# Fifteen short series of matmuls of different forms, added behind the last block of a three-stage chain

## The chip, the cores and the metric

The kernel runs on one core of a Trainium2 chip. The number that counts is the device time of one execution in microseconds (us). The engines are named as the profile names them: PE multiplies matrices (PEld is its loading of weights), ACT and DVE work on elements, POOL too, and SP issues the DMA transfers.

## The reference

Three stages follow each other. The first is attention over channels, the other two are gated layers over 12032 tokens of 256 numbers.

```python
B, N, C = (2, 6016, 256)
qn = q / (norm(q, axis=1) + 1e-06)
kn = k / (norm(k, axis=1) + 1e-06)
a = softmax(kn.transpose(0, 2, 1) @ qn / tau)      # 256 x 256, per batch
x = (v @ a).reshape(B * N, C)

h = x @ w_in                                       # 256 -> 2048
x = (h - tanh(h)) @ w_out                          # 2048 -> 256

gate = sigmoid(x @ w_gate)                         # 256 -> 1536
out = (gate * (x @ w_val)) @ w_out2                # 1536 -> 256
```

## The kernel before

The tokens of the two batches are cut into 24 blocks: eleven of 512 tokens and one of 384 in each batch. A block's tokens are the columns of the matmuls, so nearly all of them have 512 columns and those of a batch's last block 384. An accuracy near float32 is reached with operands in two parts: a high part and a low part, both float32r (a float32 that PE takes in one pass), and three products for each tile: high by high, low by high, high by low. So every product of a block stands in the trace as a group of six matmuls with six loads of 128 columns of weights.

The work of a block goes through five kinds of matmul group: `h` (lines L298 to L301, v by the product of attention weights and w_in), `x` (L341 to L344, by w_out), `ga` and `va` (L376 to L379, by w_gate and w_val) and `o` (L405 to L408, by w_out2). ACT and DVE work between them: the tanh polynomial behind `h`, the sigmoid and the product behind `ga` and `va`, and each time the split into parts.

The order on every engine is the order in which the code is written: the kernel switches the scheduler off (`tc.manual_schedule()`) and walks through steps `T`; in each it emits a unit of block p's `h` and `x`, a unit of block p-1's `ga`, `va` and `o`, and whatever else was put down for that step. Behind the last step of the last block only the loop's end follows. There the last `o` group (`p_11`, L405 to L408) is copied out of PSUM, one half by ACT (L419) and one by DVE (L420), and each half is sent to memory by an own transfer (L422). That copy is `ob`.

Pools hand out the tiles. `psw` takes one of four PSUM banks in turn, `rr` one of six float32r tiles, `mk` one of two bf16 tiles, and `v4_p` one of three large tiles for v, converted weights and outputs. A tile that takes the place of an older one waits for whoever still uses that.

At the start, batch 0's attention weights are computed from native float32 operands (L507, L455, 256 columns): the trace shows two matmul records for each such matmul in the code. Batch 1's later tiles of tokens take float32r products of 256 columns (L173 to L175).

Of the kernel before, what the change touches and what calls it, by code (L numbers as in the profile page):

```python
# [15 lines left out]
AX = mybir.AxisListType  # L16

P = 128
# h - tanh(h) = h^3 (C2 ((h^2 + CB)^2 + CG)) to 5e-7 for |h| <= HT; beyond HT the difference itself.
HT = 0.25  # L20
_C0, _C1, C2 = 0.33333317, -0.13328699, 0.051975
CB = _C1 / (2.0 * C2)
# [4 lines left out]
def kernel(  # L27
# [56 lines left out]
    def rr(name, shape=(P, 512)):  # L84
        return rr_p.tile(list(shape), F32R, tag="rr", name=name)
# [7 lines left out]
    make_identity(nc, ident)  # L93

    def warm(n, name):
        """Matmuls that only keep the PE's clock up while it would wait."""
        o = psw(name, (P, P))
        for _ in range(n):
            MM(o, ones, ones, start=True, stop=True)

    aw_hi = [wp.tile([P, NK, 2 * P], F32R, name=f"awh{i}") for i in range(N1 // 2)]
    # until batch 0's a @ w_in is there, its low part's place holds w_in
    win = [wp.tile([P, NK, 2 * P], F32, tag=f"awl{i}", name=f"win{i}") for i in range(N1 // 2)]
    aw_lo = {}
    w1_hi = [wp.tile([P, 2, C], F32R, name=f"w1h{i}") for i in range(N1 // 2)]
# [1 line left out]
    win_d = dr_p.tile([N1 // 2, P, NK, 2 * P], F32, name="win_d")  # L107

    def conv(src, shape, pool, tag, name, w=None, hi=None, lo=None):
        """float64 words to float32 (w), or to its two float32r parts (hi, lo): three stages."""  # L110
        a, m = shape
        st = pool.tile([P, a, 2 * m], U32, tag=tag, name=f"st_{name}")
        nc.sync.dma_start(out=st, in_=src)
        yield
        words = st.rearrange("p a (m t) -> p a m t", t=2)
        low, high = words[:, :, :, 0], words[:, :, :, 1]
        bt = cv(f"cb_{name}", (P, a, m))
        pt = cv(f"cp_{name}", (P, a, m))
        bu, pu = bt.bitcast(U32), pt.bitcast(U32)
        lf = low.bitcast(F32)  # L120
        nc.scalar.activation(bt, high.bitcast(F32), AF.Abs)
        nc.scalar.activation(lf, low, AF.Copy, scale=2.0**-52)
        yield 1
        nc.vector.tensor_scalar(bt, bt, 2.0**-15, 122879.9921875, ALU.max, ALU.min)
        nc.vector.tensor_scalar(
            bu, bu, 0x07FFFFFF, 3, ALU.bitwise_and, ALU.logical_shift_left
        )
        nc.vector.scalar_tensor_tensor(
            out=bu, in0=high, scalar=0xC0000000, in1=bu, op0=ALU.bitwise_and, op1=ALU.bitwise_or
        )  # L130
        nc.vector.tensor_scalar(pu, bu, 0xFF800000, None, ALU.bitwise_and)
        nc.gpsimd.tensor_tensor(out=pt, in0=lf, in1=pt, op=ALU.mult)
        yield
        if w is not None:
            nc.vector.tensor_tensor(out=w, in0=bt, in1=pt, op=ALU.add)
        else:
            nc.scalar.activation(hi, bt, AF.Copy)
            nc.gpsimd.tensor_tensor(out=bt, in0=bt, in1=hi.bitcast(F32), op=ALU.subtract)
            nc.gpsimd.tensor_tensor(out=lo, in0=bt, in1=pt, op=ALU.add)

    def whole(g):
        """Only the stages of conv."""
        for x in g:
            if x is None:
                yield
# [12 lines left out]
        src = words(w_out)[i * 256:(i + 1) * 256, :].rearrange("(a p) d -> p a d", p=P)  # L158
        return conv(src, (2, C), v4_p, "v4", f"w1{i}", hi=w1_hi[i], lo=w1_lo[i])

# [1 line left out]
    kq = {}  # L162
    acc = {}

# [1 line left out]
        kq[b] = psw(f"kq{b}", (P, 2, C))  # L166

    def s_mm(b, hi, lo, first, last):
        """hi, lo: [P, 2 (q, k), C] of one tile of tokens."""
        for ct in range(2):  # L170
            cs = slice(ct * P, (ct + 1) * P)
            o = kq[b][:, ct, :]
            MM(o, hi[:, 1, cs], hi[:, 0, :], start=first and ct == 0, stop=False, skip_group_check=True)  # L173
            MM(o, hi[:, 1, cs], lo[:, 0, :], start=False, stop=False, skip_group_check=True)
            MM(o, lo[:, 1, cs], hi[:, 0, :], start=False, stop=last, skip_group_check=True)  # L175
# [1 line left out]
    aT, nrm, ks = {}, {}, {}  # L177

    def norm_mm(b, sq, sk, first, last):
        """Column sums of the tiles of sq (of q's squares) and sk (of k's), on c's partition."""  # L180
        for o, xs in ((0, sq), (2, sk)):
            for i, x in enumerate(xs):
                for ct in range(2):
                    MM(nrm[b][:, o + ct, :], x[:, ct * P:(ct + 1) * P], ones[:, :NW],
                       start=first and o + i + ct == 0, stop=last and i == len(xs) - 1, skip_group_check=True)

    def s_softmax(b, sq, sk):
        """sq, sk: tiles whose column sums are the sums of squares of q and k."""
        np_ = nrm.get(b)
        if np_ is None:  # L190
            np_ = nrm[b] = psw(f"n{b}", (P, 4, NW))
# [5 lines left out]
        nc.vector.tensor_scalar_add(rn, rn, 1e-6)  # L197
        nc.vector.reciprocal(rn, rn)
        nc.vector.tensor_scalar(rn[:, 2:4], rn[:, 2:4], rtau[:, 0:1], None, ALU.mult)
        # q's factors as rows, the same on every partition: by the ones' product with their diagonal matrix  # L200
        dg = (cv if b else wk)(f"dg{b}", (P, 2, P))
        for ct in range(2):
            nc.vector.tensor_scalar(dg[:, ct, :], ident, rn[:, ct:ct + 1], None, ALU.mult)
# [47 lines left out]
            aT[b] = (hi, lo)  # L251

    def aw_chunk(b, i, w):
        """Rows c of a @ w_in, columns of chunk i."""
        ap_ = psw(f"aw{b}_{i}", (P, 2, 2 * P))
        parts = [(aT[b], w)] if b == 0 else [(aT[b][0], w[0]), (aT[b][1], w[0]), (aT[b][0], w[1])]
        for n, (x, y) in enumerate(parts):
            for ct in range(2):
                for kk in range(2):
                    MM(ap_[:, ct, :], x[:, kk, ct * P:(ct + 1) * P], y[:, kk, :],  # L260
                       start=n + ct + kk == 0, stop=n == len(parts) - 1 and kk == 1, skip_group_check=True)
        yield
        if b == 0:
            aw_lo[i] = wp.tile([P, NK, 2 * P], F32R, tag=f"awl{i}", name=f"awl{i}")
        nc.scalar.activation(aw_hi[i], ap_, AF.Copy)
        nc.vector.tensor_tensor(out=aw_lo[i], in0=ap_, in1=aw_hi[i].bitcast(F32), op=ALU.subtract)  # L266

# [1 line left out]
    vn = {}  # L269

    def load_v(p):
# [76 lines left out]
    def emit_x2(p):  # L348
        n = blocks[p][2]
        xp = xps.pop(p)  # L350
        if p:
            h = one_p.tile([P, 2, TB], F32R, tag="x2h", name=f"x2h{p}")
            lo = one_p.tile([P, 2, TB], F32R, tag="x2l", name=f"x2l{p}")
            h, lo = ([t[:, d, :] for d in range(2)] for t in (h, lo))
        else:
            # block 1's come before the last use of block 0's: these are where aT, acc and s1_split's are at other times
            h = [one_p.tile([P, TB], F32R, tag=t, name=f"x2{t}") for t in ("aT", "acc")]
            lo = [sx_p.tile([P, TB], F32R, tag="sx", name=f"x2l0_{d}") for d in range(2)]
        for d in range(2):
            nc.scalar.activation(h[d][:, :n], xp[d][:, :n], AF.Copy)  # L360
            nc.vector.tensor_tensor(
                out=lo[d][:, :n], in0=xp[d][:, :n], in1=h[d][:, :n].bitcast(F32), op=ALU.subtract
            )
        x2[p] = (h, lo)
# [56 lines left out]
            for d in range(NK):  # L421
                nc.sync.dma_start(out=dst[:, d], in_=o[:, d])  # L422

    # Batch 1's first J0 tiles of tokens, where the PE would wait: native float32 products of
    # what is loaded; their squares are summed later.
    JA, J0, GS = 20, 32, 5
    ks_d = dr_p.tile([2, P, 2 * C], F32, name="ks_d")
    qk1 = [x[1, 0:J0 * P, :].rearrange("(p j) c -> p j c", p=P) for x in (q, k)]
# [33 lines left out]
        nc.scalar.activation(t, epool[0][:, 0:2, :].rearrange("p a c -> p (a c)"), AF.Copy)  # L462
        nc.sync.dma_start(out=ks_d[g], in_=t)

# [1 line left out]
    rtau = const.tile([P, 1], F32, name="rtau")  # L466
    cb_t = const.tile([P, 1], F32, name="cb")
    ct_t = const.tile([P, 1], F32, name="ct")
# [10 lines left out]
    with tc.tile_pool(name="boot1", bufs=1) as boot1, tc.tile_pool(name="boot4", bufs=4) as boot4, \  # L479
# [28 lines left out]
                       start=j + jj == 0 and ct == 0, stop=j + jj == NT - 1, skip_group_check=True)  # L508

        def boot_squares(i):  # L510
            """Squares, summed in accb; the last chunk's are left to the matmuls."""
            j, n = chunks[i]
            raw = raws.pop(i)
            sq = boot3.tile([P, 2, JB, C], F32, tag="sq", name=f"sq{i}")
# [11 lines left out]
        wait, live = {}, []  # L526

        def load(i):
            """Chunk i of q and k, and what of w_in is converted along with it."""
            if i < NCH:  # L530
                load_raw(i)
            if i in (2, 5, 8, 11):
# [21 lines left out]
        nc.scalar.activation(dummy, ones[:, 0:1], AF.Sqrt)  # L554
        while live:
            live = [g for g in live if next(g, live) is None]
        # the softmax's stages, and in between what does not wait for them: two of w_in's
        # conversions, v's first parts, batch 1's first products
        sm0 = s_softmax(0, *sq)
        tv = split_v(0)  # L560
        for step in (tail[0], sm0, sm0, tail[0], sm0, tv, e_mm, e_mm, e_mm, sm0, sm0, tv, tail[1],
# [19 lines left out]
            h, lo = ((wg_hi[i], wg_lo[i]), (wv_hi[i], wv_lo[i]))[which]  # L581
        return conv(src, (2, 2 * P), v4_p, "v4", f"m{which}{i}", hi=h, lo=lo)

# [1 line left out]
    sraw = {}  # L585

    def s1_load(j):
# [40 lines left out]
        nc.vector.tensor_tensor(out=ks[1], in0=ks[1], in1=t, op=ALU.add)  # L628

    def s1_sum():  # L630
        """The sum over a group of tiles to that over all."""
        nc.vector.tensor_tensor(out=ks[1], in0=ks[1], in1=kq[1], op=ALU.add)

# [1 line left out]
    bg = {}  # L635

    def at(step, fn, *a):
        bg.setdefault(step, []).append((fn, a))

    # GV0: the steps of block 0's column tiles of w_gate and w_val; OFF..: those of the others', from  # L640
    # the first step of the block after
    GV0 = (20, 21, 22, 24, 25, 27, 28, 30, 31, 33, 34, 35)
    OFF1 = (4, 5, 7, 8, 9, 11, 12, 13, 14, 15, 16, 17)
    OFFS = (3, 4, 5, 7, 8, 9, 11, 12, 13, 15, 16, 17)
# [58 lines left out]
    for T in range(-4, (NB + 1) * N1 + 18):  # L703
# [42 lines left out]
                emit_out(u[0])  # L746
        if e0 and e0[1] == (4 if T < N1 else 12) and e0[0] + 1 < NB:
            load_v(e0[0] + 1)
    ms.__exit__(None, None, None)


# [31 lines left out]
```

## Time and profile before

| what | value |
|---|---|
| time, median of 2 runs | 2437.05 us (2436.18 to 2437.92) |
| profiled execution, span from first to last instruction | 2436.4 us |
| PE busy in the span | 2372.4 us, 97% |
| DVE, ACT, POOL busy | 1841.3 us, 1606.9 us, 259.6 us |
| mean granted TensorE clock | 0.991 |

The span stands 0.65 us under the median of the runs, within what the two runs differ by (1.74 us). For the profiled execution no other time than its span is given, so differences in the span are taken as differences in the time. Matmul records overlap: a record of 512 columns is about 0.39 us long, and the next begins 0.23 us after it. So what a matmul costs is read from start to start, or from a count over a stretch without gaps, not from the length of its record.

### The profile page before, as it was taken

Reading aid. Unit: us, or ns where it says so; the run is one execution under the profiler, and the core shown is the slowest. Engines: PE = TensorE matmul, PEld = TensorE weight load, DVE = VectorE, ACT = ScalarE, POOL = GpSimd, SP = SyncE. Lnnn points to the kernel's source line nnn. Section 1 sums busy time; section 2 is a strip of 40 time slices with the busy share of each in tenths; the row PEclk is TensorE's granted clock in tenths of the full one; section 3 lists DMA queues with packets and bytes.
Section 4 is the critical chain, followed back from the end, with each engine's and each line's share of the span. In section 5 each row is a group of like instructions: output and inputs, shape, how many; then the busy total and the mean of one; then the engine's idle time right before and its main releaser. Section 6 shows DMA issues by size and latency. Waiting matters only on the chain.

```text
span 2436.4 us, 29276 instructions
## 1 busy us (share of the span) xinstructions
PE 2372.4 (97%) x10408; PEld 1935.4 (79%) x10408; DVE 1841.3 (76%) x2791; ACT 1606.9 (66%) x2820; POOL 259.6 (11%) x171
## 2 busy tenths in 40 slices
PE   7868899999999999999999999999999999999999
PEld 6656678878888888788888888888888888888888
DVE  7899977778777777777777777777777777777764
ACT  4766666676766676776666766666666666666663
POOL 6466600111100000000000000000000000000000
PEclk9899999999999999999999999999999999999999
DMA  7432210111110110000100000000000000000000
GB/s 280 139 117 96 74 35 22 39 35 31 52 35 5 44 35 5 18 10 10 44 5 18 16 1 18 18 1 18 18 1 18 18 1 18 18 1 16 1 9 16
DMA packets 49106, 82.62 MB, mean 34 GB/s; under 512 B 4416, under 2 KB 18496, under 8 KB 48960
## 3 DMA queue, kind: packets, MB, share of 16 engines
q1 hardware_dynamic: 48960, 80.76, 10.0%
q8 instruction: 81, 1.33, 0.2%
q14 instruction: 65, 0.53, 0.1%
HBM read 65.80 MB, written 14.94 MB: 33 GB/s over the span
## 4 chain that ended last, share of the span: by engine, by line
PE 87%; DVE 7%; issue 3%; ACT 2%; POOL 1%; DMA 0%; SPq 0%; DVEq 0%; POOLq 0%; ACTq 0%
PE h L298 7%; PE x L344 7%; PE h L301 7%; PE h L299 7%; PE x L342 6%; PE x L341 6%; PE o L406 5%; PE o L405 5%; PE ga L377 5%; PE o L408 5%; PE ga L376 5%; PE va L377 5%; PE va L376 5%; PE va L379 5%; PE ga L379 5%
## 5 line engine op out<-in xcount | busy, mean ns | idle before, releaser
L314 DVE SCALAR_TENSOR_TENSOR w<-u,h 128x512 f32<-128x512 f32 (+1 forms) x384 | 259.1, 675 | 345.5 <-ACT t L310 345.1
L309 ACT ACTIVATE u<-h 128x512 f32<-128x512 f32 (+1 forms) x384 | 223.4, 582 | 256.7 <-PE h L301 256.4
L317 DVE COPY_PREDICATED w<-m,t 128x512 f32<-128x512 uint16 (+1 forms) x384 | 318.3, 829 | 41.0 <-DVE w L316 1.8
L298 PE MATMUL h<-vTh,awh 128*128 128x512 f32 (+1 forms) x768 | 303.8, 396 | 2.7 <-DVE t L315 1.9
L299 PE MATMUL h<-vTh,awl 128*128 128x512 f32 (+1 forms) x768 | 301.0, 392 | 4.2 <-DVE awl L266 4.2
L312 ACT ACTIVATE s<-u,cb 128x512 f32<-128x512 f32 (+1 forms) x384 | 274.0, 713 | 0.0
L313 ACT ACTIVATE m<-u,ct 128x512 bf16<-128x512 f32 (+1 forms) x384 | 272.3, 709 | 0.0
L316 DVE SCALAR_TENSOR_TENSOR w<-s,w 128x512 f32<-128x512 f32 (+1 forms) x384 | 264.3, 688 | 0.0
L315 DVE TENSOR_TENSOR t<-h,t 128x512 f32<-128x512 f32 (+1 forms) x384 | 258.0, 672 | 0.0
L301 PE MATMUL h<-vTl,awh 128*128 128x512 f32 (+1 forms) x768 | 237.6, 391 | 0.0
L310 ACT ACTIVATE t<-h 128x512 f32<-128x512 f32 (+1 forms) x384 | 223.7, 582 | 3.5 <-DVE w L314 0.8
L377 PE MATMUL va<-x2h,wvl 128*128 128x512 f32 (+1 forms) x552 | 216.2, 392 | 0.0
L377 PE MATMUL ga<-x2h,wgl 128*128 128x512 f32 (+1 forms) x552 | 216.1, 392 | 0.0
L376 PE MATMUL ga<-x2h,wgh 128*128 128x512 f32 (+1 forms) x552 | 215.9, 391 | 0.1
L376 PE MATMUL va<-x2h,wvh 128*128 128x512 f32 (+1 forms) x552 | 215.8, 391 | 0.0
L388 DVE TENSOR_TENSOR sg<-va,sg 128x512 f32<-128x512 f32 (+1 forms) x288 | 191.9, 666 | 19.7 <-PE va L379 18.8
L387 ACT ACTIVATE sg<-ga 128x512 f32<-128x512 f32 (+1 forms) x288 | 168.8, 586 | 16.6 <-PE ga L379 12.5
L379 PE MATMUL va<-x2l,wvh 128*128 128x512 f32 (+1 forms) x576 | 178.5, 391 | 0.0
L379 PE MATMUL ga<-x2l,wgh 128*128 128x512 f32 (+1 forms) x576 | 178.0, 390 | 0.0
L298 PEld LDWEIGHTS h<-vTh,awh 128*128 128x128 f32 x768 | 145.2, 189 | 36.6 <-DVE t L315 4.4
L299 PEld LDWEIGHTS h<-vTh,awl 128*128 128x128 f32 x768 | 144.9, 189 | 35.9 <-DVE awl L266 7.5
L301 PEld LDWEIGHTS h<-vTl,awh 128*128 128x128 f32 x768 | 144.2, 188 | 33.3
(396 smaller groups left out, 4772.0 us busy)
## 6 DMA issues: line engine op xcount, KB each, us to landing
v<-in_v_dram SPq DMA_DIRECT2D x22, 512.0 KB, 4.2
out_dram<-ob SPq DMA_DIRECT2D x22, 512.0 KB, 3.0
sr<-in_q_dram SPq DMA_DIRECT2D x47, 128.0 KB, 2.3
sr<-in_k_dram SPq DMA_DIRECT2D x47, 128.0 KB, 2.6
raw<-in_q_dram SPq DMA_DIRECT2D x13, 384.0 KB, 8.1
raw<-in_k_dram SPq DMA_DIRECT2D x13, 384.0 KB, 8.2
st_wi<-in_moe_w_in_dram SPq DMA_DIRECT2D x8, 512.0 KB, 7.3
er<-in_q_dram SPq DMA_DIRECT2D x16, 256.0 KB, 2.6
```

Source lines behind the costliest of these rows:

```text
L298: MM(o[:, :n], aw_hi[i][:, kk, fs], h[:, kk, :n], start=kk == 0, stop=False)
L299: MM(o[:, :n], aw_lo[i][:, kk, fs], h[:, kk, :n], start=False, stop=False)
L301: MM(o[:, :n], aw_hi[i][:, kk, fs], lo[:, kk, :n], start=False, stop=kk == 1)
L312: nc.scalar.activation(s, u, AF.Square, bias=cb)
L313: nc.scalar.activation(m, u, AF.Relu, bias=ct2)
L314: nc.vector.scalar_tensor_tensor(out=w, in0=u, scalar=C2, in1=hp, op0=ALU.mult, op1=ALU.mult)
L315: nc.vector.tensor_tensor(out=t, in0=hp, in1=t, op=ALU.subtract)
L316: nc.vector.scalar_tensor_tensor(out=w, in0=s, scalar=CG, in1=w, op0=ALU.add, op1=ALU.mult)
L317: nc.vector.copy_predicated(w, m.bitcast(U16), t)
L376: MM(o[:, :n], wht[m // 2][:, d, ms], h[d][:, :n], start=d == 0, stop=False)
L377: MM(o[:, :n], wlt[m // 2][:, d, ms], h[d][:, :n], start=False, stop=False)
L379: MM(o[:, :n], wht[m // 2][:, d, ms], lo[d][:, :n], start=False, stop=d == 1)
```

## The change

Behind the loop, 172 matmuls in fifteen series are added, fourteen of 12 and one of 4. They read weights that are in SBUF anyway, a bf16 tile of ones, a float32r tile of zeros and a float32 tile of 0.5; they write to banks of `psw`, and nothing reads these sums. Three instructions prepare the tiles: two memsets on DVE and one Copy with scale 0 on ACT. The other edits remove comments and docstrings. The output is computed as before.

```diff
         if e0 and e0[1] == (4 if T < N1 else 12) and e0[0] + 1 < NB:
             load_v(e0[0] + 1)
+
+    bones = mk_p.tile([P, 512], BF16, tag="mk", name="bones")
+    nc.vector.memset(bones, 1.0)
+    zero = rr("zero")
+    nc.scalar.activation(zero, bones, AF.Copy, scale=0.0)
+    flat = lambda t: t.rearrange("p a c -> p (a c)")
+    mv = [flat(w1_hi[0]), flat(w1_lo[0]), flat(w2_hi[0]), flat(w2_lo[0])]
+    wt = [wg_hi[0][:, 0, :P], wg_lo[0][:, 0, :P], wv_hi[1][:, 1, :P], wv_lo[1][:, 1, :P]]
+
+    def probe_same():
+        o = psw("probe_same")
+        for i in range(12):
+            MM(o, wt[0], mv[0], start=i == 0, stop=i == 11)
+
+    def probe_turns():
+        o = psw("probe_turns")
+        for i in range(12):
+            MM(o, wt[i % 4], mv[i % 3], start=i == 0, stop=i == 11)
+
+    def probe_banks():
+        o = [psw("probe_banks") for _ in range(2)]
+        for i in range(12):
+            MM(o[i % 2], wt[i % 4], mv[i % 3], start=i < 2, stop=i > 9)
+
+    def probe_bf16():
+        o = psw("probe_bf16")
+        for i in range(12):
+            MM(o, bones[:, :P], bones, start=i == 0, stop=i == 11)
+
+    def probe_rows64():
+        o = psw("probe_rows64")
+        for i in range(12):
+            MM(o[:64], wt[i % 4][:, :64], mv[i % 3], start=i == 0, stop=i == 11)
+
+    def probe_rows32():
+        o = psw("probe_rows32")
+        for i in range(12):
+            MM(o[:32], wt[i % 4][:, :32], mv[i % 3], start=i == 0, stop=i == 11)
+
+    def probe_zero():
+        o = psw("probe_zero")
+        for i in range(12):
+            MM(o, zero[:, :P], zero, start=i == 0, stop=i == 11)
+
+    def probe_cols(n):
+        o = psw(f"probe_cols{n}")
+        for i in range(12):
+            MM(o[:, :n], wt[i % 4], mv[i % 3][:, :n], start=i == 0, stop=i == 11)
+
+    def probe_later(n):
+        o = psw(f"probe_later{n}")
+        for i in range(12):
+            MM(o[:, :n], wt[i % 4], mv[i % 3][:, 512 - n:], start=i == 0, stop=i == 11)
+
+    def probe_native():
+        o = psw("probe_native")
+        for i in range(4):
+            MM(o, ones, flat(vn_probe)[:, :512], start=i == 0, stop=i == 3)
+
+    vn_probe = v4_p.tile([P, NK, 512], F32, tag="v4", name="vprobe")
+    nc.vector.memset(vn_probe, 0.5)
+    probe_same()
+    probe_turns()
+    probe_banks()
+    probe_bf16()
+    probe_rows64()
+    probe_rows32()
+    probe_zero()
+    for n in (504, 500, 480, 448, 400, 320):
+        probe_cols(n)
+    probe_later(496)
+    probe_native()
     ms.__exit__(None, None, None)
```

On PE the series stand behind the last `o` group and ahead of the branch that ends the program; shown is the start of them. A name ahead of the arrow is the tile written, those behind it are the operands, and the last number is the output's size.

```order
 L406 MATMUL o_21170<-p_11h,w2l_573 128x384
 L408 MATMUL o_21170<-p_11l,w2h_567 128x384 x2
-L779 UNCONDITIONAL_BRANCH
+L761 MATMUL probe_same<-w1h_116,wgh_538 128x512 x12
+L766 MATMUL probe_turns<-w1h_116,wgh_538 128x512
+L766 MATMUL probe_turns<-w1l_124,wgl_544 128x512
+L766 MATMUL probe_turns<-w2h_562,wvh_551 128x512
+L766 MATMUL probe_turns<-w1h_116,wvl_557 128x512
```

Nothing ahead of the last `o` group changes its place on PE; the series take the place directly behind it. On DVE, where both memsets are added, the end of the program reads so:

```order
 L323 TENSOR_TENSOR p_11l<-sg_11_21447,p_11h 128x384
 L420 COPY ob_21460<-o_21170 128x384
-L779 UNCONDITIONAL_BRANCH
+L751 MEMSET bones 128x512
+L809 MEMSET vprobe 128x1024
+L851 UNCONDITIONAL_BRANCH
```

Both memsets come behind the copy of the last output's second half (L420), so that the copy and its transfer keep their places.

## Rows read from the trace of the kernel before

**Rows 1.** The page: busy time of PE, and its slices of the span.

```profile
PE 2372.4 (97%) x10408; PEld 1935.4 (79%) x10408; DVE 1841.3 (76%) x2791; ACT 1606.9 (66%) x2820; POOL 259.6 (11%) x171
...
PE   7868899999999999999999999999999999999999
...
PEclk9899999999999999999999999999999999999999
```

**Rows 2.** The chain that ended last, its end: start us, us, what.

```profile
2430.45 0.53 ACT p_11h L322
2430.98 0.04 issue
2431.02 0.44 PE o L405
...
2431.99 0.36 PE o L408 x2
2432.35 0.02 issue
2432.37 0.50 ACT ob L419
2432.87 0.02 issue
2432.89 0.56 DVE ob L420
```

**Rows 3.** Timeline of all engines, the last instructions: start us, us, engine, line.

```profile
2431.82 0.51 PE L408 MATMUL o<-p_11l,w2h 128*128 128x384 f32 x2
...
2432.89 0.94 SPq L422 DMA_DIRECT2D out_dram<-ob  x2
2432.89 0.56 DVE L420 COPY ob<-o 128x384 f32<-128x384 f32 x1 [1.34 <-ACT ob L419]
```

**Rows 4.** DMA from 2430 to 2437 us: busy tenths in 40 slices.

```profile
DMA  0000000000000000000004994997000000000000
```

**Rows 5.** Stretches: us, busy (x count) of PE, PEld, DVE, ACT, POOL; PEclk; DMA.

```profile
1800.00:2000.00 200.00, 200.00 (x862) 161.55 (x861) 146.19 (x226) 130.97 (x228) 0.00 (x0) 1.00 0.03 11
2000.00:2200.00 200.00, 200.00 (x861) 161.57 (x860) 145.93 (x226) 131.34 (x228) 0.00 (x0) 1.00 0.03 11
2400.00:2430.00 30.00, 30.00 (x175) 30.00 (x174) 10.54 (x20) 9.64 (x19) 0.00 (x0) 1.00 0.00 1
```

**Rows 6.** Timeline of PE in the last block, columns as in rows 3.

```profile
2424.38 0.34 PE L376 MATMUL ga<-x2h,wgh 128*128 128x384 f32 x1
...
2427.50 0.34 PE L376 MATMUL ga<-x2h,wgh 128*128 128x384 f32 x1
```

**Rows 7.** Timeline of PE, six float32r matmuls of 256 columns and the one behind.

```profile
656.28 0.28 PE L173 MATMUL kq<-sh 128*128 128x256 f32 x1
...
656.99 0.40 PE L298 MATMUL h<-vTh,awh 128*128 128x512 f32 x1
```

**Rows 8.** Timeline of PE, native float32 matmuls of 256 columns, equal ones merged.

```profile
4.37 2.05 PE L507 MATMUL kq<-raw 128*128 128x256 f32 x4 [0.81 <-DMA raw<-in_k_dram]
...
46.73 1.67 PE L507 MATMUL kq<-raw 128*128 128x256 f32 x7
62.77 1.94 PE L184 MATMUL n<-ones,accb 128*128 128x64 f32 x8 [14.37 <-DVE accb L523]
...
70.27 2.77 PE L455 MATMUL kqe<-er 128*128 128x256 f32 x6
```

**Rows 9.** Stretches round the pause of PE at 48 us, and at the end.

```profile
53.00:62.00 9.00, 0.00 (x0) 0.00 (x0) 8.83 (x12) 4.48 (x6) 2.80 (x2) 0.50 0.45 166
70.20:72.90 2.70, 2.70 (x9) 2.16 (x8) 1.96 (x4) 2.69 (x6) 0.00 (x0) 0.50 0.00 0
2433.00:2435.00 2.00, 0.00 (x0) 0.00 (x0) 0.45 (x1) 0.00 (x0) 0.00 (x0) 1.00 0.53 197
2435.20:2436.40 1.20, 0.00 (x0) 0.00 (x0) 0.00 (x0) 0.00 (x0) 0.00 (x0) 0.50 0.00 0
```

**Rows 10.** Groups by line, a memset on DVE: count, busy us, mean ns.

```profile
L91 DVE MEMSET ones<- 128x128 f32 x1 | 0.2, 165 | 0.8 <-PEq L765 0.8
```

## The prediction

> **What bounds the kernel now.** I read the page first: PE is busy for 97% of the span and at the full clock but for the first slices [rows 1]. For this change only the end counts, so I went on to the chain of waits there. It runs through the last `o` group on PE, the copy of its first half by ACT and of its second by DVE [rows 2]. Behind that copy comes the second transfer, and DMA is busy until slice 28 of 40, about 2435.0 us [rows 4]; the span ends at 2436.4. So 1.4 us of waits and barrier follow the last transfer. On PE the two last matmuls begin at 2431.82 and, since a record of 384 columns is 0.34 us long and both together take 0.51, at 2431.99 [rows 3, 6]. Their step, start to start, is 0.173 us (below), so PE could begin another matmul at 2432.17. From there to the span's end it has 4.2 us in which it does nothing.
>
> **What the change does to that end.** Nothing ahead of the last `o` group moves, and the output's copies and transfers stand ahead of the new DVE and ACT instructions. So the output leaves as before. The 172 new matmuls begin at 2432.17, and the program's end waits for PE's last instruction as for that of every engine. The first 4.2 us of them are hidden behind the output's way out, and the rest lengthens the span one to one. The price is thus the sum of the steps.
>
> **The steps.** In the two dense stretches nearly all matmuls have 512 columns; 200 us hold 862 and 861 records, one of which began earlier, hence 200/861 = 0.2323 us each [rows 5]. In the last block the 18 matmuls from one `ga` group to the next take 2427.50 - 2424.38 = 3.12 us, 0.1733 us at 384 columns [rows 6], as 30/174 = 0.172 says too [rows 5]. Six float32r matmuls of 256 columns take 656.99 - 656.28 = 0.71 us, 0.118 us each [rows 7]. Native float32 at the full clock: seven records take 1.67 us, of which the last is about 0.38, so the step is 1.29/6 = 0.215 us [rows 8]. The first chunk holds one tile of tokens, two matmuls in the code, and shows four records [rows 8]; a native matmul of 256 columns thus costs two records, 0.430 us, and one of 512 columns twice that, 0.860 us.
>
> **The sum.**
> The series of 512 float32r columns with 128 output rows and full weights (same, turns, banks, zero) are 48 matmuls at 0.2323: 11.15 us. That weights are the same each time, banks change or operands are zero shows in no row; I take the body's step for all, and 0.215 (512 columns streamed as the native records do it) as the lower end.
> Those with 64 and 32 output rows are 24 more at 0.2323: 5.58 us. No row of the trace has fewer than 128 output rows. Below lies again 0.215, above the native price 0.860; I take the body's, since the same 512 columns are streamed and the trace prices by columns.
> The six column counts: between the three measured steps I draw straight lines. That gives 0.146 for 320, 0.181 for 400, 0.203 for 448, 0.218 for 480, 0.227 for 500 and 0.229 for 504, together 1.202 us, times 12: 14.43 us. The twelve matmuls of 496 columns from a later start cost 0.225 each: 2.70 us.
> The bf16 series: no bf16 matmul is in the trace. I take 0.215, the step of a record that streams 512 columns in two passes: 12 x 0.215 = 2.58 us. Half of that (0.118, as many bytes as 256 float32r columns) is the lower end; 0.2323 with a weight load of 0.118 that isn't hidden (rows of 256 columns show loads no slower than that), 0.35 or 4.2 us in all, the upper.
> The native series is 4 x 0.860 = 3.44 us.
> Together 11.15 + 5.58 + 14.43 + 2.70 + 2.58 + 3.44 = 39.9 us. PE's last record ends some 0.16 us behind its step (0.34 against 0.173), at 2432.17 + 39.9 + 0.16 = 2472.2. Behind it comes the barrier. In the profile of before, 1.4 us lie between the last transfer's landing and the end; a part of that is the queue's check of transfers that are then long done, so between 0.6 and 1.4, and I take 0.9. The new span is 2473.1 us, 36.7 longer. With the median of the runs instead of the span: **2473.8 us**, a factor of 1.015.
>
> **What I cost at nothing.** The two memsets take about 0.3 to 0.7 and 1.3 us, by 0.165 us for 128 columns [rows 10], and run from 2433.45, when DVE has copied `ob` [rows 2]. They are needed by the bf16 series after 36 matmuls, at about 2440.5, and by the native one at about 2469; ACT's Copy is needed by the zero series, near 2449. The cover is 6 us or more. If it were gone, PE would wait 2 us at most. Each series takes a bank of `psw` that a series or group four banks back wrote, so its first matmul waits for a matmul that ended at least two series before. I cost this at nothing; were the pipeline emptied each time, it would cost up to 0.16 us (record less step) at eleven places, 1.8 us. The clock stays up: in 30 us of the last block it is 1.00 with PE busy throughout [rows 5], and it fell only after PE had stood idle from 2432.3 to past 2435.0 [rows 9].
>
> **The rivals.**
> *The step of the body is not that of the series.* In the body ACT and DVE read and write beside PE; behind the last block they are idle. If the 0.2323 us were theirs, the series would run at 0.215 per 512 columns, 0.42 ns a column: 72 matmuls 15.5, the column counts 13.4, the later start 2.5, with bf16 and native 37.4 us in all, 2.5 less: 2471.3 us. Against it: in the last block ACT and DVE are busy a third of the time instead of two thirds [rows 5], and 384 columns still cost 0.1733, 0.45 ns a column. The Trainium skill ("TensorE: Matmul & The Clock Gate", section on the back-to-back issue gap) gives columns / 2.4 GHz plus 2.5 ns, 0.2158 us for 512 columns, without naming the operand's type; the native records agree with that, the float32r rows of the body do not, and by the page alone the time would be this rival's.
> *A slow form.* This one ends more than 2% slower. All float32r rows before have 128 output rows and 256, 384 or 512 columns. If those with 64 and 32 rows were taken at the native price, 24 x (0.860 - 0.232) = 15.1 us are added: 2488.9 us, 2.1% over before. If it were the column counts that are no multiple of 128, then 12 x (2652 + 496) columns at 1.68 ns (0.430 / 256) make 63.5 us in place of 17.1: 2520 us. It decides from one such pair of series on. For it speaks only that no row excludes it; against it, that the trace prices three column counts near one line.
> *The half clock.* After 14.4 us of idleness PE's clock was 0.50, the 1.2 GHz level, and native records then came (2.77 - 0.63)/5 = 0.427 us apart instead of 0.215 [rows 8, 9]. Were the series to run so, the sum would double to 79 us: about 2513 us. Against it: PE would have to stand idle first, and the longest cover that could break is the 2 us above.
> *Pauses between the series.* Emptied pipelines and late semaphores at the eleven bank waits, 0.16 to 0.4 us each, add 2 to 4 us: 2476 to 2478.
> *Not slower.* If the unread sums were left out, or the program's end did not wait for PE, the time stays 2437. The built program has all series in PE's order, ahead of the branch.
>
> **How the numbers follow.** Sum as worked out 0.68; body's step not that of the series 0.12; pauses 0.10; slow form 0.06; half clock 0.02; not slower 0.02. The first three end between 2471 and 2478, which is the range. About 2% either way, 48.7 us, is what a measurement of this kernel can tell from no change; the first three and the last are within it. Slower by more than 2% is a slow form or the half clock, 0.08; faster by more than 2% has no mechanism, and gets 0.01; within 2% gets 0.91. The forecast itself is a time 1.5% longer, inside that bound.
>
> **What would show it.** In the profile after: the first of the series begins within 0.1 us of 2432.17; the copies and transfers of `ob` stand where they stood; PE has no idle time over 0.1 us before a series, and the clock is 1.00 until the end; 11 steps of a 512-column series take 2.56 us; a series of 320 columns 1.6 us, one of bf16 2.4 us; from the end of the last record to the end of the span 0.6 to 1.4 us. The prediction is wrong if one of the forms unseen before (64 or 32 rows, bf16, odd column counts) has a step far from its line, or if the ends of the span are set by something other than PE.

## The result and the profile after

The kernel with the fifteen series takes 2474.45 us (median of two runs, 2474.05 and 2474.86) against 2437.05: a ratio of 1.0149, 95% interval 1.013 to 1.0168, so 37.4 us more. Forecast were 2473.8 us, between 2471 and 2478.

The page of the kernel after, the same parts as in [rows 1]:

```profile
PE 2412.7 (98%) x10584; PEld 1965.7 (80%) x10584; DVE 1843.9 (75%) x2793; ACT 1610.5 (65%) x2821; POOL 259.9 (11%) x171
...
PEclk9899999999999999999999999999999999999999
```

PE is busy 40.3 us longer (2412.7 - 2372.4), and its clock stays up to the end. The records grew by 176: 168 of fourteen series, and eight for the four native matmuls.

The chain that ended last in the kernel after (start us, us, what) answers to [rows 2]:

```profile
2431.20 0.35 PE o L408 x2
2431.54 2.81 PE probe_same L761 x12
2434.35 2.78 PE probe_turns L766 x12
2437.13 2.79 PE probe_banks L771 x12
2439.92 2.60 PE probe_bf L776 x12
2442.53 2.78 PE probe_rows L781 x12
2445.30 2.77 PE probe_rows L786 x12
2448.07 2.74 PE probe_zero L791 x12
2450.81 14.44 PE probe_cols L796 x72
2465.25 2.71 PE probe_later L801 x12
2467.96 3.43 PE probe_native L806 x8
```

Before, the chain went from the last `o` group to the copies by ACT and DVE; now it stays on PE. Between the fifteen series there is no "issue" piece, so no pause. Added up they take 39.85 us, and the last one ends at 2471.39; the span ends 0.9 us later, at 2472.3. That the end waits for PE stands among the waits of the queue that issues the transfers (us in total, times, longest); before, that queue's wait at the end was for the output's transfer alone, 1.5 us:

```profile
SPq L851 <- PE probe_native L806: 36.3, 1, 36.3
```

The timeline of the same kernel round the last `o` group answers to [rows 3]:

```profile
2431.03 0.51 PE L408 MATMUL o<-p_11l,w2h 128*128 128x384 f32 x2
2431.38 2.97 PE L761 MATMUL probe_same<-w1h,wgh 128*128 128x512 f32 x12
...
2432.10 1.37 SPq L422 DMA_DIRECT2D out_dram<-ob  x2
2432.11 0.56 DVE L420 COPY ob<-o 128x384 f32<-128x384 f32 x1 [1.33 <-ACT ob L419]
...
2433.36 0.91 DVE L809 MEMSET vprobe<- 128x1024 f32 x1 [0.16 <-issue]
```

The first series follows the last `o` matmul after a step of 0.18 us (2431.38 - 2431.20), the copy and the transfers of `ob` keep their distance to it, and the three preparing instructions end at 2434.3, over 5 us ahead of their first use at 2439.8. All of it stands 0.8 us earlier than in the profile of before, which is the difference of two executions: behind the same `o` group, the stretch to the span's end was 4.4 us and is now 41.1 (2472.3 - 2431.20), forecast 41.1 (0.17 + 39.9 + 0.16 + 0.9).

### The profile page after: what moved, and what is told of

Same layout as the page of the kernel before. It is cut to its first block, busy times and chain, and to the rows that moved or that the text cites. A ratio compares the mean times of both kernels' runs of the same rounds, so it can differ in the third digit from the quotient of the medians.

```text
span 2472.3 us, 29636 instructions
## 1 busy us (share of the span) xinstructions
PE 2412.7 (98%) x10584; PEld 1965.7 (80%) x10584; DVE 1843.9 (75%) x2793; ACT 1610.5 (65%) x2821; POOL 259.9 (11%) x171
## 4 chain that ended last, share of the span: by engine, by line
PE 87%; DVE 6%; issue 3%; ACT 2%; DMA 1%; POOL 1%; SPq 0%; DVEq 0%; POOLq 0%; ACTq 0%
PE h L298 7%; PE h L299 6%; PE h L301 6%; PE x L344 6%; PE x L342 6%; PE x L341 6%; PE o L406 5%; PE ga L377 5%; PE o L405 5%; PE ga L376 5%; PE va L376 5%; PE va L377 5%; PE va L379 5%; PE o L408 5%; PE ga L379 5%
## 5 line engine op out<-in xcount | busy, mean ns | idle before, releaser
L317 DVE COPY_PREDICATED w<-m,t 128x512 f32<-128x512 uint16 (+1 forms) x384 | 318.7, 830 | 41.1 <-DVE w L316 1.8
L298 PEld LDWEIGHTS h<-vTh,awh 128*128 128x128 f32 x768 | 145.1, 189 | 36.7 <-DVE t L315 4.4
```

The costliest lines, as they stand in the source:

```text
L298: MM(o[:, :n], aw_hi[i][:, kk, fs], h[:, kk, :n], start=kk == 0, stop=False)
L317: nc.vector.copy_predicated(w, m.bitcast(U16), t)
```

## Experiments

**e1_same12 and e2_same24: how much of PE's work the end hides.** Only the first series stands behind the last block, with 12 or with 24 matmuls.

```diff
     ms.__exit__(None, None, None)   # of the kernel before, ahead of it:
+    o = psw("probe_same")
+    for i in range(12):             # e2: 24
+        MM(o, wt[0], mv[0], start=i == 0, stop=i == 11)
```

> Only the series with one pair of operands stands behind the last block: 12 matmuls, 2.8 us. Theory (PE's free 4.2 us at the end hide the first matmuls): PE ends ahead of the last transfer, the stretch from the last o matmul's start to the span's end stays 4.4 us, and the time stays within 1 us of 2437.05. Rival (each added matmul lengthens the time, because the program's end waits for PE on its own): 7.2 us for that stretch, and 2.8 us more.

> The same series with 24 matmuls, 5.6 us, longer than the 4.2 us that PE has free. Theory: from the last o matmul's start to the span's end 0.17 + 24 x 0.2323 + 0.16 + 0.9 = 6.8 us instead of 4.4, so 2.4 us more. Rival (one to one): 10.0 us and 5.6 more. If all unread matmuls were free: 4.4.

Measured: e1 1.0003 of the kernel before (0.9994 to 1.0012), e2 1.0009 (1.0 to 1.0018). The timeline of e1, and then that of e2, whose spans are 2436.5 and 2438.9 us:

```profile
2431.86 0.51 PE L408 MATMUL o<-p_11l,w2h 128*128 128x384 f32 x2
2432.20 2.97 PE L756 MATMUL probe_same<-w1h,wgh 128*128 128x512 f32 x12
```

```profile
2431.89 0.52 PE L408 MATMUL o<-p_11l,w2h 128*128 128x384 f32 x2
2432.25 5.79 PE L756 MATMUL probe_same<-w1h,wgh 128*128 128x512 f32 x24
```

In e1 PE ends at 2435.17, about when the output's second transfer lands (2435.0 by the DMA slices), and the end comes 1.3 us later: from the last `o` matmul's start (2432.03) to the span's end 4.4 us, as without the series. In e2 PE ends at 2438.04 and the end follows 0.9 us later: 6.8 us (2438.9 - 2432.07), as worked out. So matmuls behind the last block are free as long as PE's end and the 0.9 us behind it stay within the output's way out, and from there cost one to one. Of e2's 5.62 us, 2.4 us lengthened the span, so 3.2 us were hidden. One to one from the first on is refuted; the times, 0.1 and 2.1 us over before, say the same.

**e3_twice: the sum doubled.**

```diff
+    for _ in range(2):
     probe_same()
...
     probe_native()
```

> All fifteen series twice over. Theory (the steps add up and nothing else counts): the second pass costs its full 39.9 us, 2474.45 + 39.9 = 2514.4 us, with the clock at 1.00 throughout. Rival (part of the price was paid once: a start, an end, pauses at the first use of a form): less than 2512. Rival (a longer run of such matmuls brings the clock down): more than 2520.

Measured: 2514.03 us, 1.0313 (1.0299 to 1.0327), 39.6 us over the kernel with one pass; 2514.4 were expected. In the chain of e3 the second pass begins at 2471.80 and its last series ends as follows:

```profile
2471.80 2.81 PE probe_same L761 x12
...
2508.24 3.43 PE probe_native L806 x8
```

2508.24 + 3.43 - 2471.80 = 39.87 us. Nothing was paid only once, and the clock stayed at 1.00.

**e4_in_the_pause: matmuls where PE waits.**

```diff
+                warm(60, "warm1")
                 nrm[0] = psw("n0", (P, 4, NW))
                 norm_mm(0, *([accb[:, x, 0]] for x in range(2)), True, False)
```

> The kernel before with 60 unread matmuls of ones (native float32, 128 columns, about 12.9 us) put not at the end but where PE waits 14.4 us for DVE at 48 us. Theory (a matmul costs what PE's exposed time costs): nothing is added, PE still goes on at 62.8 us, and since it did not stand idle the clock stays at 1.00 there instead of 0.50 from 52.6 to 73.1 us, which takes 1 to 3 us off: 2434 to 2437. Rival (any 13 us of PE work is added to the time): 2450. Rival (the pause was not free, for instance because SBUF or the queue is shared): over 2439.

Measured: 2436.8 us, 0.9997 (0.9988 to 1.0006). PE's timeline in e4, beside [rows 8]:

```profile
49.35 13.56 PE L99 MATMUL warm<-ones 128*128 128x128 f32 x120
63.13 1.08 PE L184 MATMUL n<-ones,accb 128*128 128x64 f32 x8 [0.22 <-DVE accb L523]
```

13.6 us of added PE work cost nothing that can be measured: PE still goes on when DVE is done, 0.36 us later than in the profile of before, and the next eight matmuls take 1.08 us instead of 1.94, at a granted clock of 0.98 between 62.7 and 68 us instead of 0.50. The expectation that the clock stays up was met only in part: PE waited again for 2.3 us, and the clock was 0.50 from 68 to 70 us in e4 too, and 0.79 from 70 to 73 (0.50 before). What all this gave back, 1.1 us at the first token product (77.33 instead of 78.41), is less than the interval. The rivals of 2450 and of over 2439 fall.

**e5_forms: values or type.** The prediction priced the bf16 series apart from the others. Eight series of 24 with other values show why it is shorter.

```diff
+    series("d_ones", lambda i: (one[:, :P], one))
+    series("d_nil", lambda i: (nil[:, :P], nil))
+    series("d_nilw", lambda i: (nil[:, :P], mv[0]))
+    series("d_nilx", lambda i: (wt[0], nil))
+    series("d_bf16", lambda i: (bw[:, :P], wide))
```

> Eight series of 24 matmuls of 512 columns behind the last block, each with other values or another type: real weights and tokens' factors (d_same), float32r ones (d_ones), float32r zeros (d_nil), zero weights with real moving data (d_nilw), real weights with zero moving data (d_nilx), bf16 copies of real data (d_bf16), real data on 64 input rows (d_half), weights and moving data of one tile (d_own). The question is what makes a float32r step of 512 columns 0.232 us where the bf16 series had 0.216. Theory (the type does): all float32r series 0.226 to 0.235, bf16 with real data 0.216. Rival (the values do, and bf16 was short for its ones): d_ones and d_nil near 0.216, d_bf16 with real data near 0.232. Rival (two tiles read at once get in each other's way): d_own, d_ones and d_nil short, the others long.

The chain of e5 (start us, us of 24 matmuls):

```profile
2432.87 5.62 PE d_same L767 x24
2438.50 5.45 PE d_ones L767 x24
...
2449.39 5.44 PE d_nilw L767 x24
2454.83 5.62 PE d_nilx L767 x24
2460.45 5.20 PE d_bf L767 x24
2465.64 5.80 PE d_half L767 x24
2471.44 5.68 PE d_own L767 x24
```

This kernel and those of e6, e8 and e10 to e12 were timed once each, so only steps within their profiles are read, at a granted clock of 1.00. Per step: 0.234, 0.227, 0.227 (d_nil), 0.227, 0.234 and, for bf16 with real data, 0.217 with a first step of 0.227 and then 0.216. So the type makes 0.011 us, and values make nothing: zeros as moving data with w_gate's weights cost as much as real ones, and zero weights as little as ones. Two tiles read at once are not the cause either: d_nilw reads two and has the short step. The last two series begin with a step of 0.34 us, where the number of input rows changes from 128 to 64 and back; behind it d_half has 0.234, so half the input rows save nothing, and d_own 0.228. That left 0.007 us between series of the same type, for which the place of the operands was a suspect.

**e6_narrow: fewer columns.**

```diff
+    for n in (288, 256, 224, 192, 160, 128, 64, 384, 512):
+        cols(n)          # 24 matmuls each
```

> Nine series of 24 float32r matmuls with other column counts than the change had. Theory (the price goes by columns down to the weights' load, which is a floor): 288 columns 0.132 us, 256 columns 0.118, and 224, 192, 160, 128 and 64 columns all about 0.108 to 0.12, the time in which 128 columns of weights load. Rival (columns alone): 0.104, 0.090, 0.076, 0.062 and 0.034 us. Rival (a slow form under 256 columns, at the native price): 192 columns 0.32 us.

Stretches of e6 from the first matmul of 224 and of 64 columns to the next series (us, PE busy, PEld busy):

```profile
2437.66:2440.33 2.67, 2.67 (x27) 2.67 (x25) 0.00 (x0) 0.00 (x0) 0.00 (x0) 1.00 0.00 0
2448.32:2450.97 2.65, 2.65 (x27) 2.65 (x26) 0.00 (x0) 0.00 (x0) 0.00 (x0) 1.00 0.00 0
```

By 24: 0.111 and 0.110 us; 256 columns took 0.118 and 288 took 0.132. From 224 columns down to 64 the step stays at 0.111. That the load of 128 columns of weights is this floor was argued and is not shown: PEld is busy all the time, but so it is at 288 columns, above the floor, and no series had few columns and fewer weights. Columns alone and the slow form are refuted.

**e7_align and e8_starts: the start within 64 bytes.** The weights of w_gate, w_val and w_out2 and v's parts begin 32 bytes off a multiple of 64, since a small tile of 32 bytes stands before them; w_out's and the zeros don't.

```diff
-        rn = one_p.tile([P, 4], F32, tag="rn", name=f"rn{b}")
+        rn = one_p.tile([P, 16], F32, tag="rn", name=f"rn{b}")[:, :4]
```

> The kernel before without any added series; one small tile (rn, four numbers a partition) takes 64 bytes instead of 32, so that the tiles behind it (v's parts and the weights wgh to w2l), which began 32 bytes off a multiple of 64, begin at multiples of 64. Theory (where a float32r operand's bytes begin sets 3 to 11 ns of a 512-column step, as the forms' series showed 0.227 us with weights that begin at such a multiple and 0.231 to 0.238 with those that don't): the body's 8334 steps of 512 columns, 0.2327 us on average, come down to between 0.227 and 0.230, 22 to 47 us less, 2390 to 2416 us. Rival (the place in memory counts in another way, or the weights' slices do): 2436 to 2439, unchanged. Rival (PE's gain is eaten by waits for DVE): above 2425 with PE idle time grown.

> Nine series of 24 float32r matmuls of 480 columns behind the last block, all of two tiles that begin at multiples of 64 bytes; weights and moving data begin 0, 4, 8 or 16 numbers (0, 16, 32, 64 bytes) into them (w0x0, w4x0, w8x0, w16x0, w0x4, w0x8, w0x16, w8x8), and one has 32 output rows (m32). Theory (32 bytes off a multiple of 64 is the cost): w0x0, w16x0 and w0x16 0.212 to 0.214 us flat, w8x0 and w4x0 0.216 to 0.220, w0x8 and w0x4 longer too or equal. Rival (it is the distance of the two tiles, not the start): all alike. m32: if the load of 128 columns of weights makes the 10 ns that are left over the 0.216 of bf16 (0.203 at 480 columns), then near 0.204, else as w0x0.

e7 measured 2432.84 us, 0.9979 (0.997 to 0.9988): faster, clear of noise, but by 5 us and not by 22 to 47. A stretch of its body beside [rows 5]:

```profile
1800.00:2000.00 200.00, 200.00 (x863) 161.92 (x862) 145.44 (x224) 131.04 (x227) 0.00 (x0) 1.00 0.03 11
```

200/862 = 0.2320 us a step instead of 0.2323. In e8 the 480-column series took 0.216 to 0.220 us wherever they began, with 32 output rows too (5.20 us for 24), although a load of 32 columns has a record of 108 ns instead of 188. The theory that the start within a tile costs 3 to 11 ns fell, and the load as the cause of the remaining 0.011 us with it.

**e9_both: the pause filled and the tile of 64 bytes.** The edits of e4 and e7 together.

> The kernel before with the 60 matmuls of ones in PE's pause and the small tile of 64 bytes together, no series at the end. Theory (each takes its own: 1 us by the clock after the pause, 5 us by shorter steps): 2431 to 2433 us against 2438. Rival (the start is held by other engines and the pause's gain was noise): as with the tile alone, 2432.8.

Measured: 2431.92 us, 0.9974 (0.9965 to 0.9984). That is faster than both kernels; beyond e7 alone it is 0.0005 of the time, within the intervals, so that the two gains add is not shown.

**e10_pairs and e11_align_series: distance, place or alternation.**

```diff
+    for a, c in ((0, 0), (0, 1), (0, 2), (0, 3), (0, 4), (0, 6), (4, 4), (4, 5), (4, 6), (4, 0)):
+        series(f"p{a}w{c}", w1_hi[c], w1_hi[a])
+    series("far", aw_hi[0], w1_hi[0])
+    series("far2", wg_hi[0], w1_hi[4])
```

> Twelve series of 24 float32r matmuls of 512 columns behind the last block. Moving data is the first or the fifth tile of w_out's high parts (2048 bytes apart each), weights come from the same or another tile of them (p0w0, p0w1, p0w2, p0w3, p0w4, p0w6, p4w4, p4w5, p4w6, p4w0), or from far ones (far: attention product's, far2: w_gate's). What is open is why a step is 0.2266 us in some series and 0.231 to 0.238 in others with the same values and type, now that the start within 64 bytes is out. Theory (the distance between the two tiles): p0w0 as p4w4, p0w1 as p4w5, p0w2 as p4w6, with p0w0 at 0.2266 and others longer. Rival (the weights' place alone): p0w4 as p4w4, p0w6 as p4w6, p0w0 as p4w0. Rival (neither; the phase at which a series begins): no such pairs, and changes inside a series.

> The kernel with the small tile of 64 bytes, so that w_gate's tiles begin at multiples of 64, and seven series of 24 matmuls of 512 columns behind it: one pair of w_out's tiles (a_one, again at the end as a_last), w_gate's weights with the same moving data (a_gate), two weights in turn (a_wts of w_out, a_gwts of w_gate), two moving tiles in turn (a_mov), and the change's four weights and three moving tiles in turn (a_turn). Theory (the start of the weights within 64 bytes sets the step as long as one pair repeats, and the alternation of tiles sets it otherwise, so that the body gained little by the alignment): a_one, a_gate, a_last 0.2267, a_wts, a_gwts, a_turn 0.230 to 0.233. Rival (w_gate's place in memory, not its start): a_gate 0.231 to 0.238 as before, a_wts 0.2267. Rival (the start alone): all seven 0.2267.

The chain of e10, all pairs of w_out's tiles merged by the moving tile, and then four series of e11's chain:

```profile
2431.72 32.68 PE p0w L755 x144
2464.39 21.76 PE p4w L755 x96
```

```profile
2427.67 5.46 PE a_one L755 x24
2433.13 5.59 PE a_gate L755 x24
2438.71 5.46 PE a_wts L755 x24
...
2455.22 5.51 PE a_turn L755 x24
```

The timeline of e10, its last series:

```profile
2491.43 5.78 PE L755 MATMUL far<-w1h,wgh 128*128 128x512 f32 x24
```

In e10 every pair takes 0.227 us (32.68/144, 21.76/96), whatever the distance; with w_gate's weights the last series took 0.234 (5.78 less the last record's overhang of 0.16, by 24), with the attention product's 0.227. In e11 w_gate's weights, now at a multiple of 64 bytes, still take 0.233 (5.59/24), and two weights in turn cost no more than one (a_wts 0.227, a_gwts 0.233). So the distance and the alternation of two tiles don't set it; w_gate's place remains. It is not the whole account: a_turn, with four weights and three moving tiles in turn, took 0.230, and the same turn in the change, where these weights begin 32 bytes off, 0.232 (2.78/12).

**e12_places: which place.** Values of w_out and w_gate are copied to other places.

```diff
+    series("b_low", low, m0)          # w_gate's values at byte 103680
+    series("b_high", high, m0)        # w_out's values at byte 224640
+    series("b_mhigh", m0, high)
+    series("b_both", flat(wg_hi[0]), high)
```

> Twelve series of 24 matmuls of 512 columns behind the kernel with the small tile of 64 bytes; the values are w_out's or w_gate's, copied to tiles at other places. Weights from: w_out's tile at byte 50432 (b_out), w_gate's at 155008 (b_gate), w_gate's values at 103680 (b_low) and 115968 (b_mid), w_out's values at 224640 (b_high), tiles at 134400, 138496, 142656 and 146752 (b_x2h, b_x2l, b_vth, b_vtl), all with the moving data at 50432; then that weight with moving data at 142656 (b_mvth) and 224640 (b_mhigh), and both far up (b_both). Theory (a place from some byte between 118000 and 155000 on costs 5 to 6 ns a step, whatever is in it): b_out, b_low, b_mid 0.2267, b_gate, b_high 0.231 to 0.235, the change somewhere among the four between. Rival (the values or the tile's own layout): b_low as b_gate, b_high as b_out. For moving data the same question is open: b_mhigh 0.2267 if only the weights' place counts, over 0.230 if either does.

The chain of e12:

```profile
2427.01 5.49 PE b_out L765 x24
2432.50 5.59 PE b_gate L765 x24
2438.09 5.45 PE b_low L765 x24
...
2448.99 5.59 PE b_high L765 x24
...
2460.03 5.44 PE b_x2l L765 x24
2465.46 5.60 PE b_vth L765 x24
...
2476.66 5.51 PE b_mvth L765 x24
2482.17 5.58 PE b_mhigh L765 x24
2487.75 5.45 PE b_both L765 x24
```

With the moving data at byte 50432, weights up to byte 138496 (b_x2l) cost 0.227 us a step (0.229 in the first series), and from 142656 on (b_vth) 0.233, whatever their values. The theory was half right: with moving data and weights both far up (b_both) the step is 0.227 again. In these series weights and moving data on different sides of a place between those two bytes cost 0.003 us (b_mvth, moving data at 142656: 0.230) to 0.006 us. Only one pair with both far up was run.

## Why the prediction was right

**What sets the end.** The step held that the series begin 0.17 us behind the last `o` matmul, that the output's way out hides a part of them, and that the rest counts one to one. The profile after shows the first, e1 and e2 the hidden part and where it ends, and e3 the one to one. The size of the hidden part is put wrongly in the prediction's words: of the 4.2 us in which PE had nothing to do, 3.2 hide matmuls (39.85 - 36.7 here, 5.62 - 2.4 in e2), since PE's last record outlasts its step by 0.16 and 0.9 us follow it. The sum has both terms, so its 36.7 us were right; 39.9 less 4.2 would have been 35.7.

**The sum.** 39.9 us were worked out, 39.85 measured, and it was not a balance of large errors: the four series with full output rows 11.12 (11.15 forecast), 64 and 32 rows 5.55 (5.58), the six column counts 14.44 (14.43), the later start 2.71 (2.70), bf16 2.60 (2.58), native 3.43 (3.44). Straight lines between three column counts were enough for six others: each of the six, from start to start, came within 0.002 us a step. The body's 0.2323, taken for all full series, is a mean over groups of 0.229 (`x`) to 0.234 (last section); that the series' own mixture came to the same is in part luck, since single series of that form lay between 0.227 and 0.234 (e5).

**The end behind PE.** 0.9 us were taken between 0.6 and 1.4, and 0.9 came (e2 the same). The reason given, a check of transfers by the queue, is timed by no run by itself; what the runs show is 0.9 us behind PE's last record and about 1.4 behind the last transfer.

**Span and time.** The new span is 35.9 us longer (2472.3 - 2436.4), the time of that execution, 2474.05, stands 1.75 us above it, and the median went up by 37.4. The body of this execution was 0.8 us shorter than that of before; with that the lengthening is the 36.7 forecast, but the sign that the first series begins within 0.1 us of 2432.17 failed as written (2431.38). The rest is what executions differ by, and that the median came within 0.7 us of the forecast is in part luck: 27 of the kernel before, timed beside e1 to e4, lie between 2436.22 and 2439.07.

**Costs put at nothing.** The memsets took 0.48 and 0.91 us and were done over 5 us before they were needed. The bank waits cost nothing visible: no piece between two series. The clock stayed at 1.00.

**The rivals.** That the body's step was ACT's and DVE's doing is refuted: behind the last memset, which ends at 2434.3, both are idle, and the next 24 matmuls (turns and banks) took 5.57 us, 0.232 each. The rule of the Trainium skill ("TensorE: Matmul & The Clock Gate", section on the back-to-back issue gap), columns / 2.4 GHz plus 2.5 ns, which that section gives as the gap of an isolated matmul, agrees here with bf16 (0.216 at 512 columns in e5) and, if a record counts twice its columns, with native float32 (3.43/8 = 0.429 us for 512 columns in the change), and not with float32r, which took 0.227 to 0.234. The slow form, the half clock and the pauses did not come. "Not slower" holds for the first twelve matmuls alone (e1).

## What to carry to other kernels

Price added matmuls by start-to-start steps of the same type at the nearest column counts, draw a line between them, and subtract only the time for which PE stood free at that place, less what the end needs behind PE: 13.6 us in a pause cost nothing, 40 us at the end cost 36 to 37. Below 224 columns a float32r matmul with 128 columns of new weights gets no cheaper. Dummy work behind the last output is free only until it outlasts that output's copies and transfers (here 3.2 us of steps).

## What the runs showed that was not expected

In single series, a float32r step of 512 columns is 0.227 us where weights and moving data lie on the same side of a place between bytes 138,496 and 142,656 of a partition, and 0.230 to 0.234 where they don't (e12; e5 and e10 fit). In this kernel `h` (weights low, v's parts at 142,624 and above) and `ga`, `va` and `o` (weights from 154,976 on, moving data below) have their operands on different sides, `x` on one. PE's timeline in the kernel before, and then in e7, shows one `h` and one `x` group of six, by the starts of their first matmuls:

```profile
1906.71 0.40 PE L298 MATMUL h<-vTh,awh 128*128 128x512 f32 x1
...
1908.11 0.39 PE L341 MATMUL x<-g_12h,w1h 128*128 128x512 f32 x1
...
1909.49 0.39 PE L405 MATMUL o<-p_8h,w2h 128*128 128x512 f32 x1
```

```profile
1900.95 0.40 PE L298 MATMUL h<-vTh,awh 128*128 128x512 f32 x1
...
1902.33 0.40 PE L341 MATMUL x<-g_12h,w1h 128*128 128x512 f32 x1
...
1903.72 0.39 PE L405 MATMUL o<-p_8h,w2h 128*128 128x512 f32 x1
```

Before, `h` takes 1.40 us and `x` 1.38; in e7 1.38 and 1.39. Means of the steps between 1500 and 2200 us, before and in e7: `h` 0.2331 and 0.2309, `x` 0.2290 and 0.2313, `ga` 0.2340 and 0.2338, `va` 0.2344 and 0.2321, `o` 0.2336 and 0.2326. So before, `x` is the shortest, as the place would have it, but not at 0.227; and in e7 it is no shorter than `h`, although the operands of `x`, allocated ahead of the enlarged tile, did not move. Times the steps in 22 blocks (2112 of `h` and of `x`, 1584 of each other kind) the differences add up to the 5 us that e7 gained: 10 us saved, 5 lost in `x`.

If v's parts and the tiles of `x2` changed places, `h`, `ga` and `va` would have both operands on one side: 5280 steps at 4 to 5 ns, by the distance to `x` in the kernel before, an estimate of some 25 us. It was not tried, and by e7, where `x` has no such lead over `h`, it may be far less. Nor is it shown what stands behind that place, why `x` lost in e7, or why the whole float32r step is 0.011 us above bf16's.
